# Tile 0's six projections beside the MLP's end: six whole accumulators in place of 24 single units

## The chip, the cores and the metric

The kernel runs on one core of a Trainium2 chip. The metric is the device time of one execution in microseconds. The times given are medians over several executions of the same program.

## The reference

The program adds two branches over the same input `x` of 2048 rows and 512 columns, mixed by a gate.

```python
g = sigmoid((x * gate_w).sum(-1, keepdims=True))
a = A(x, mem0, Wq, Wk, Wv, Wo, seg_len=32)      # recurrent attention with memory, 32 heads of 128
b = gelu(layernorm(x) @ w1 + b1) @ w2 + b2      # MLP, 512 -> 1376 -> 512
return g * a + (1 - g) * b

# A: for each of the 64 segments of 32 rows
h = concat([mem, xs])                           # 8 memory rows + 32 rows of x
q, k, v = h @ Wq, h @ Wk, h @ Wv                # 32 heads of 128 each
o = softmax(mask(q k^T * scale)) v @ Wo
mem, out = o[:8], o[8:]                         # the memory goes on to the next segment
```

The 64 segments are strictly one after the other, because each needs the memory rows of the one before. The MLP has no such order.

## The kernel before

**Two parts, one after the other.** The first part is the whole MLP with the gates. The second part is the recurrent attention, segment by segment. Both are written out under a manual schedule: each engine runs its instructions in the order in which the program text issues them, and the framework adds the waits.

**The MLP's loop.** Rows are taken in 16 tiles of 128, two tiles to a block, so there are 8 blocks (`NBLK`). The hidden width of 1376 is cut into 11 chunks (`FC`, the last of them with 96 rows). The loop over `u` has 88 steps, one for each pair of block and chunk. A step issues `up(u)` (four matmuls of 128 x 256 on L456 into `hp`, which has two buffers, and a Gelu on ScalarE, L461, into `hg`), and then `down(u - 2)` (two matmuls of 128 x 512 on L473 into the accumulators `bp`). At chunks 5 and 7 a step also transposes a normalised tile on TensorE (L445, `tp`). When a block's last `down` is done, VectorE (L476) and ScalarE (L481) write its two rows of `c_all`. The last ScalarE write at the MLP's end releases the first matmul of the second part (L360, the mask).

**A segment in the second part.** The array holds 32 rows of a segment. To use it well, projections are column-tiled: `qk_unit` and `v_unit` issue four matmuls with 32 columns of weights each (L211, L222; 128 rows by 32 columns, moving 512 elements) to the four column groups of the array. One such group of four is called a unit here. An accumulator (one bank of 128 x 512) is complete after four units, one for each 128 rows of the 512-long contraction (`KC` = 4).

**The leftover rows of tile 0.** Only 24 of a segment's 32 rows ride with the 8 memory rows in one column group of 32. The 8 remaining rows of each of the four segments of a tile are gathered into `GL`, 32 rows for a tile, and projected for the whole tile ahead of time: two accumulators for V (`left_v`, `vb` = 0 and 1) and four for Q and K (`left_qk`). In the second part, this work for tile T+1 is filled in during tile T by a generator. For tile 0 it has to be done before the second part starts. This is what `setup()` does. It is a generator, and the MLP's loop calls `next(pre, None)` once per step in the last three blocks (`u` from 55).

- First, `setup()` transposes the memory `m0` with four small matmuls (L488) and gathers the rows with GpSimd (`x_left`, `prep_h`).
- `left_v(0, vb)` yields after each unit. Once complete, an accumulator is written to `vt` by ScalarE (L282), stored to the DRAM tile `vd` by a DMA issued by SyncE (L285), and, after the second one, read back in another order into `vs` by 16 small DMAs (L292). `vt` has one buffer.
- `left_qk(0, t, hf)` yields after each unit too. VectorE then transposes the accumulator (L217) into `Tt` (two buffers in this part), and GpSimd copies it into `QL` (L264) or `KL` (L268).
- `left_v_in(0)` copies `vs` to `VL` on GpSimd (L299).

All six accumulators use one bank of PSUM, since `side()` has one bank here (`nside` = 1). The evacuation is put in a queue by `later` and issued by `flush`, which is called one step of the generator after the last unit. Before it hands out the bank again, `side()` flushes whatever is still queued. With 24 unit yields, six yields after the flushes and one at the start, `setup()` runs from u = 55 to u = 86. Step 87 calls it no more.

**DMA queue.** SyncE issues nearly all DMAs in program order. The second half of `Wo` (L138) is issued in step 74, because it overwrites the staged input `x_all`; it stands in SyncE's order behind the 16 reads of `vs`.

Of the kernel before, what the change touches and what calls it, by code (L numbers as in the profile page):

```python
# [23 lines left out]
def kernel(ctx, tc, A_x, A_mem0, A_Wq, A_Wk, A_Wv, A_Wo, A_seg_len, B_x, B_w1, B_b1, B_w2, B_b2, gate_w, out):  # L24
    nc = tc.nc
    P = 128
    _, S, Dm = A_x.shape
# [109 lines left out]
    def ld_wo(h0, h1):  # L137
        nc.sync.dma_start(Wo_sb[:, h0:h1, :], A_Wo[h0:h1].rearrange("h e d -> e h d"))  # L138
# [45 lines left out]
    def flush(q, n=1):  # L184
        for _ in range(min(n, len(q))):
            k, ev = q.pop(0)
            ev()
            side_todo.discard(k)

    def later(q, ev, k):  # L190
        side_todo.add(k)
        q.append((k, ev))

    def side(shape, dtype=FP32):
        side_n[0] += 1
        n = pools["nside"]
        while side_n[0] - n in side_todo:
            flush(dve_q)
            flush(act_q)
        return bank(5 + side_n[0] % n, shape, dtype)  # L200
# [7 lines left out]
    def qk_unit(bk, G, t, h0, h1, kc):  # L208
        n = (h1 - h0) * 32
        for j in range(4):  # L210
            nc.tensor.matmul(bk[32 * j:32 * j + 32, 0:n], lhsT=G[:, kc, :], rhs=W5[t][:, kc, h0:h1, j, :],  # L211
                             start=(kc == 0), stop=(kc == KC - 1), tile_position=(0, 32 * j))

    def qk_tr(bk, h0, h1):
        n = (h1 - h0) * 32
        Tt = pools["sb"].tile([P, 512], FP32, tag="Tt", bufs=pools["nTt"], name="Tt")
        nc.vector.transpose(out=Tt[:, 0:n], in_=bk[:, 0:n])  # L217
        return Tt[:, 0:n].rearrange("p (h r) -> p h r", r=32)

    def v_unit(bk, G, vb, kc):  # L220
        for j in range(4):
            nc.tensor.matmul(bk[32 * j:32 * j + 32, :], lhsT=G[:, kc, :], rhs=Wv5[:, kc, 4 * vb:4 * vb + 4, j, :],  # L222
                             start=(kc == 0), stop=(kc == KC - 1), tile_position=(0, 32 * j))
# [20 lines left out]
    def x_left(T):  # L244
        xT = xTs[T]
        GL = xp.tile([P, KC, 32], BF16, tag="GL", name="GL")
        nc.gpsimd.tensor_copy(out=GL[:].rearrange("p k (i c) -> p k i c", c=LEFT),
                              in_=xT[:].rearrange("p k (i c) -> p k i c", c=seg)[:, :, :, RIDE:seg])
        GLs[T] = GL
# [3 lines left out]
    def left_qk(T, t, hf):  # L253
        h0, h1 = HF[hf]
        bk = side([P, 512])
        side_k = side_n[0]
        for kc in range(KC):
            qk_unit(bk, GLs[T], t, h0, h1, kc)
            if kc < KC - 1:
                yield  # L260
        def ev():
            Tv = qk_tr(bk, h0, h1)
            if t == 0:
                nc.gpsimd.tensor_copy(out=QL[T % 2][:, h0:h1, :], in_=Tv)  # L264
            else:
                for hh in range(h0 // 8, h1 // 8):
                    r0 = 8 * hh - h0
                    nc.gpsimd.tensor_copy(out=KL[T % 2][:, :, :, hh, :], in_=Tv[:, r0:r0 + 8, :].rearrange("p g (s c) -> p g s c", c=LEFT))  # L268
        later(dve_q, ev, side_k)
        yield  # L270

    def left_v(T, vb):
        bk = side([P, 512])
        side_k = side_n[0]
        for kc in range(KC):
            v_unit(bk, GLs[T], vb, kc)
            if kc < KC - 1:
                yield

        def ev():  # L280
            vt = pools["sb"].tile([P, 4, Dh], BF16, tag="vt", bufs=1, name="vt")
            nc.scalar.copy(out=vt[:].rearrange("p i e -> p (i e)"), in_=bk[:])  # L282
            if vb == 0:
                vds[T] = dr.tile([P, 4, 2, Dh], BF16, tag="vd", name="vd")
            nc.sync.dma_start(vds[T][:, 2 * vb:2 * vb + 2], vt[:].rearrange("p (a g) e -> p a g e", g=2))  # L285
            if vb == 1:
                src = vds.pop(T)[:].rearrange("(j s c) h g e -> j h c s (g e)", j=4, s=SPT)
                vs = pools["sb"].tile([P, SPT, 2, Dh], BF16, tag="vs", bufs=1, name="vs")
                for j in range(4):
                    for hh in range(4):  # L290
                        r0 = 32 * j + LEFT * hh
                        nc.sync.dma_start(vs[r0:r0 + LEFT].rearrange("p s g e -> p s (g e)"), src[j, hh])  # L292
                vls[T] = vs

        later(act_q, ev, side_k)
        yield

    def left_v_in(T):
        nc.gpsimd.tensor_copy(out=VL[T % 2][:], in_=vls.pop(T)[:])  # L299
# [48 lines left out]
    def prep_h(s):  # L348
        T, si = divmod(s, SPT)
        nc.gpsimd.tensor_copy(out=hT[s % NHT][:, :, M:32], in_=xTs[T][:, :, si * seg:si * seg + RIDE])  # L350
# [43 lines left out]
    NBLK = NT // TB  # L394
# [56 lines left out]
    def up(u):  # L451
        blk, fc = divmod(u, FC)
        rows = min(P, F - fc * P)
        hp = mps.tile([P, TB * P], FP32, tag="hp", bufs=2, name="hp")
        for kc in range(KC):
            nc.tensor.matmul(hp[:rows, :], lhsT=w1_sb[:, kc, fc * P:fc * P + rows], rhs=yTs[blk][:, kc, :], start=(kc == 0), stop=(kc == KC - 1))  # L456
        if fc == FC - 1:
            hg_ = hgl[blk % 2]
        else:
            hg_ = mwork.tile([P, TB * P], BF16, tag="hg", bufs=LAG + 2, name="hg")  # L460
        nc.scalar.activation(out=hg_[:rows, :], in_=hp[:rows, :], func=ACTF.Gelu_apprx_tanh, bias=b1_sb[:rows, fc:fc + 1], scale=1.0)  # L461
        return hg_
# [3 lines left out]
    def down(u, hg_):  # L466
        blk, fc = divmod(u, FC)
        rows = min(P, F + 1 - fc * P)
        for tt in range(TB):
            T = blk * TB + tt  # L470
            if fc == 0:
                bpt[T] = mps.tile([P, Dm], FP32, tag=f"bp{T % 4}", name="bp")
            nc.tensor.matmul(bpt[T][:], lhsT=hg_[:rows, tt * P:(tt + 1) * P], rhs=w2_sb[:rows, fc, :], start=(fc == 0), stop=(fc == FC - 1))  # L473
        if fc == FC - 1:
            T = blk * TB
            nc.vector.tensor_scalar(out=c_all[:, T, :], in0=bpt.pop(T)[:], scalar1=omg_all[:, T:T + 1], scalar2=None, op0=ALU.mult)  # L476
            c_q.append(T + 1)

    def c_act():
        for T in c_q:  # L480
            nc.scalar.activation(out=c_all[:, T, :], in_=bpt.pop(T)[:], func=ACTF.Copy, scale=omg_all[:, T:T + 1])  # L481
        c_q.clear()

    def setup():

        m0p = side([P, KC, M], BF16)
        for kc in range(KC):
            nc.tensor.transpose(m0p[:, kc, :], m0[:, kc * P:(kc + 1) * P], ident[:M, :M])  # L488
        nc.vector.tensor_copy(out=hT[0][:, :, 0:M], in_=m0p[:])
        x_left(0)  # L490
        x_left(1)
        prep_h(0)
        yield
        for vb in range(2):
            yield from left_v(0, vb)
            flush(act_q)
            yield
        for hf in range(2):
            for t in range(2):
                yield from left_qk(0, t, hf)  # L500
                flush(dve_q)
                yield
        left_v_in(0)
# [21 lines left out]
    for u in range(NBLK * FC):  # L525
        blk, fc = divmod(u, FC)
        T1 = (blk + 1) * TB
        pend.append((u, up(u)))
        if fc == 2:
            c_act()  # L530
        if len(pend) > LAG:
            down(*pend.pop(0))
        if T1 < NT:
            if fc == 1 or fc == 3:
                ys[fc // 2] = norm(T1 + fc // 2)
            elif fc == 5 or fc == 7:
                norm_tr(T1 + fc // 2 - 2, ys[fc // 2 - 2])
        if blk % 2 == 0:
            if fc in (2, 5, 6, 7) and T1 + 2 < NT:
                bn(T1 + 2 + (2, 5, 6, 7).index(fc) )  # L540
            if fc == 8 and T1 + 2 < NT:
                newton(T1 + 2, T1 + 6)

        elif fc in (2, 4, 6, 8):
            T = T1 + (fc - 2) // 2
            if T < NT:
                gates(T, T + 1)
        elif fc == 10 and T1 < NT:
            gates2(T1, T1 + 4)
        if blk == 0 and fc in (9, 10):  # L550
            gates(fc - 9, fc - 8)
        if blk == 1 and fc == 0:
            gates2(0, 2)
        if blk == 1 and fc in (1, 3):
            gates(2 + fc // 2, 3 + fc // 2)
        if blk == 1 and fc == 9:
            gates2(2, 4)
        if blk == NBLK - 2 and fc == 8:
            ld_wo(H // 2, H)
        if blk >= NBLK - 3:  # L560
            next(pre, None)
    for a in pend:
        down(*a)
# [298 lines left out]
```

## Time and profile before

| | |
|---|---|
| median of 10 executions | 838.2 us (836.77 to 838.51) |
| profiled execution, its own time | 838.28 us |
| its span in the trace | 836.5 us |
| the MLP's last three blocks with `setup()`, first `hp` matmul of u = 55 to the end of the last `bp` matmul | 62.63 to 103.99 us |
| first matmul of the second part (L360) | 104.76 us |
| TensorE busy over the span | 808.7 us (97%) |
| ScalarE, VectorE, GpSimd busy | 434.1, 502.3, 273.6 us |
| granted TensorE clock, mean | 0.998 |

Times in the trace are microseconds from the start of the span. The profiled execution took 1.78 us longer than its span, and lies 0.08 us above the median. A matmul's record is longer than its share of TensorE's time, since matmuls overlap; what a group of matmuls costs is read from start to start.

### The profile page before, as it was taken

Reading aid. Unit: us, or ns where it says so; the run is one execution under the profiler, and the core shown is the slowest. Engines: PE = TensorE matmul, PEld = TensorE weight load, DVE = VectorE, ACT = ScalarE, POOL = GpSimd, SP = SyncE. Lnnn points to the kernel's source line nnn. Section 1 sums busy time; section 2 is a strip of 40 time slices with the busy share of each in tenths; the row PEclk is TensorE's granted clock in tenths of the full one; section 3 lists DMA queues with packets and bytes.
Section 4 is the critical chain, followed back from the end, with each engine's and each line's share of the span. In section 5 each row is a group of like instructions: output and inputs, shape, how many; then the busy total and the mean of one; then the engine's idle time right before and its main releaser. Section 6 shows DMA issues by size and latency. Waiting matters only on the chain.

```text
span 836.5 us, 49253 instructions
## 1 busy us (share of the span) xinstructions
PE 808.7 (97%) x22417; PEld 494.0 (59%) x22417; DVE 502.3 (60%) x1019; ACT 434.1 (52%) x1245; POOL 273.6 (33%) x625
## 2 busy tenths in 40 slices
PE   5999999999999999999999999999999999999986
PEld 3665555666566566656655665666566656655554
DVE  5763256575666666665656565666666565656553
ACT  3554455545455555555455545555554555455542
POOL 8000134242433333243424242423333243424220
PEclk9999999999999999999999999999999999999999
DMA  9890300000001010101010100001010101010000
GB/s 307 276 377 24 103 25 15 24 16 15 25 18 28 10 36 9 37 11 35 4 31 15 29 17 21 25 18 28 10 36 11 36 10 35 4 35 6 10 5 24
DMA packets 38216, 37.64 MB, mean 45 GB/s; under 512 B 13545, under 2 KB 36434, under 8 KB 36466
## 3 DMA queue, kind: packets, MB, share of 16 engines
q1 hardware_dynamic: 37874, 34.31, 12.4%
q8 instruction: 177, 2.90, 1.4%
q14 instruction: 37, 0.30, 0.1%
q0 software_dynamic: 128, 0.13, 0.1%
HBM read 26.03 MB, written 6.29 MB: 39 GB/s over the span
## 4 chain that ended last, share of the span: by engine, by line
PE 94%; DVE 2%; DMA 1%; SPq 1%; ACT 1%; issue 1%; DVEq 0%; ACTq 0%
PE b L211 35%; PE b L233 18%; PE b L222 17%; PE b L384 5%; PE hp L456 4%; PE bp L473 4%; PE b L360 2%; PE b L369 2%; PE b L681 2%; PE b L716 1%; PE b L389 1%; PE b L670 1%; DMA Wo_sb<-in_A_x_dram 1%; PE b L320 1%; PE b L373 0%
## 5 line engine op out<-in xcount | busy, mean ns | idle before, releaser
L217 DVE STREAM_TRANSPOSE Tt<-b 128x512 f32<-128x512 f32 (+1 forms) x384 | 225.9, 614 | 86.7 <-PE b L211 72.5
L211 PEld LDWEIGHTS <-hT 128*32 128x32 bf16 x5120 | 134.8, 97 | 100.2 <-DVE hT L717 15.5
L233 PE MATMUL b<-Wo_sb,UTT 128*32 128x256 bf16 (+1 forms) x4736 | 162.7, 285 | 1.2 <-ACT UTT L616 0.8
L222 PE MATMUL b<-Wv_sb,hT 128*32 128x512 bf16 x2048 | 141.8, 378 | 0.0
L211 PE MATMUL b<-Wq_sb,hT 128*32 128x512 bf16 x2048 | 132.9, 379 | 1.4 <-DVE hT L717 1.4
L211 PE MATMUL b<-Wk_sb,hT 128*32 128x256 bf16 (+1 forms) x3072 | 133.4, 308 | 0.0
L233 PEld LDWEIGHTS <-UTT 128*32 128x32 bf16 x4736 | 121.3, 97 | 19.3 <-ACT UTT L616 1.5
L651 ACT CAST KT<-Tt 128x256 bf16<-128x256 f32 (+1 forms) x192 | 87.1, 476 | 53.9 <-DVE Tt L217 53.8
L602 POOL TENSOR_TENSOR Px<-E,R 128x256 bf16<-128x256 bf16 x64 | 43.0, 672 | 219.4 <-DVE R L686 219.4
L686 DVE RECIPROCAL R<-b 128x256 f32<-128x256 f32 x64 | 112.5, 1758 | 0.0
L651 POOL CAST QT<-Tt 128x512 bf16<-128x512 f32 x64 | 39.1, 611 | 192.2 <-DVE Tt L217 192.2
L616 ACT CAST UTT<-b 128x256 bf16<-128x256 f32 x256 | 76.9, 388 | 23.5 <-PE b L389 23.5
L705 ACT CAST wsb<-b 128x256 bf16<-128x256 f32 x66 | 24.6, 372 | 120.0 <-PE b L233 120.0
L674 DVE RECIPROCAL R<-b 128x64 f32<-128x64 f32 x64 | 35.7, 557 | 79.5 <-PE b L671 79.5
L651 ACT CAST QT<-Tt 128x512 bf16<-128x512 f32 x64 | 39.6, 619 | 65.5 <-DVE Tt L217 65.5
L384 PEld LDWEIGHTS <-V 32*128 32x128 bf16 x4096 | 35.2, 91 | 45.7 <-DVE Pm L676 31.8
L222 PEld LDWEIGHTS <-hT 128*32 128x32 bf16 x2048 | 49.5, 96 | 21.1
L461 ACT ACTIVATE hg<-hp,b_sb 128x256 bf16<-128x256 f32 x80 | 37.7, 473 | 44.8 <-PE hp L456 44.6
L685 ACT CAST UTT<-b 128x64 bf16<-128x64 f32 x128 | 20.9, 215 | 75.0 <-PE b L389 75.0
L456 PE MATMUL hp<-yT,w_sb 128*128 128x256 bf16 (+1 forms) x352 | 54.0, 278 | 3.4 <-ACT hg L461 1.6
L604 POOL TENSOR_TENSOR racc<-racc,R 128x320 f32<-128x320 f32 x64 | 55.5, 867 | 0.0
L717 DVE CAST hT<-b 128x32 bf16<-128x32 f32 x63 | 12.1, 192 | 62.0 <-PE b L716 62.0
(116 smaller groups left out, 1079.0 us busy)
## 6 DMA issues: line engine op xcount, KB each, us to landing
Wv_sb<-in_A_Wv_dram SPq DMA_DIRECT2D x4, 1024.0 KB
Wq_sb<-in_A_Wq_dram SPq DMA_DIRECT2D x4, 1024.0 KB
Wk_sb<-in_A_Wk_dram SPq DMA_DIRECT2D x4, 1024.0 KB
Wo_sb<-in_A_Wo_dram SPq DMA_DIRECT2D x2, 2048.0 KB
vd<-vt SPq DMA_DIRECT2D x32, 128.0 KB
vs<-vd SPq DMA_DIRECT2D x256, 16.0 KB
out_dram<-o SPq DMA_DIRECT2D x16, 128.0 KB
Wo_sb<-in_A_x_dram SPq DMA_DIRECT2D x1, 1024.0 KB
```

Of the source, the lines that this page charges most:

```text
L211: nc.tensor.matmul(bk[32 * j:32 * j + 32, 0:n], lhsT=G[:, kc, :], rhs=W5[t][:, kc, h0:h1, j, :], start=(kc == 0), stop=(kc == KC - 1), til ...
L217: nc.vector.transpose(out=Tt[:, 0:n], in_=bk[:, 0:n])
L222: nc.tensor.matmul(bk[32 * j:32 * j + 32, :], lhsT=G[:, kc, :], rhs=Wv5[:, kc, 4 * vb:4 * vb + 4, j, :], start=(kc == 0), stop=(kc == KC - ...
L233: nc.tensor.matmul(bk[32 * g:32 * g + 32, :], lhsT=ut[:, i, j, c0:c0 + 32], rhs=Wo_sb[:, 4 * i + j, d0:d1], start=(j == 0 and i < 4), stop ...
L384: nc.tensor.matmul(U[j][:, i, :], lhsT=V[q, i, :], rhs=Pt[q, i, c_main:c_main + n], start=(i == 0), stop=False, skip_group_check=True, til ...
L456: nc.tensor.matmul(hp[:rows, :], lhsT=w1_sb[:, kc, fc * P:fc * P + rows], rhs=yTs[blk][:, kc, :], start=(kc == 0), stop=(kc == KC - 1))
L461: nc.scalar.activation(out=hg_[:rows, :], in_=hp[:rows, :], func=ACTF.Gelu_apprx_tanh, bias=b1_sb[:rows, fc:fc + 1], scale=1.0)
L602: nc.gpsimd.tensor_tensor(out=Px[:, :, 0:32], in0=E[:, :, 16:48], in1=Rr, op=ALU.mult)
L604: nc.gpsimd.tensor_tensor(out=racc[:], in0=racc[:], in1=R[:], op=ALU.add)
L616: nc.scalar.copy(out=UTT[T % 2][:, :, j, c0 + M:c0 + 40], in_=U[:])
L651: (nc.gpsimd.tensor_copy if bi == 2 else nc.scalar.copy)(out=dst, in_=Tv)
L686: nc.vector.reciprocal(out=R[:, 8 * NG:].rearrange("p (i q) -> p i q", q=32), in_=sr)
```

## The change

The generators `left_v` and `left_qk` are run through without yielding, so all four units of an accumulator (16 matmuls) are issued one after the other, and its evacuation is flushed right behind them in the same step. The loop now calls `next(pre, None)` at every fourth step only. The yields that remain are one at the start and one for each of the six accumulators; the calls come at u = 56 (memory transposes), 60 and 64 (V), 68, 72, 76 and 80 (Q and K, in the same order as before), and 84 (`left_v_in`).

```diff
@@ setup()
         for vb in range(2):
-            yield from left_v(0, vb)
+            for _ in left_v(0, vb):
+                pass
             flush(act_q)
             yield
         for hf in range(2):
             for t in range(2):
-                yield from left_qk(0, t, hf)
+                for _ in left_qk(0, t, hf):
+                    pass
                 flush(dve_q)
                 yield
         left_v_in(0)
@@ the MLP's loop over u
-        if blk >= NBLK - 3:
+
+        if blk >= NBLK - 3 and u % 4 == 0:
             next(pre, None)
```

No instruction is added or taken away on TensorE, ScalarE, GpSimd or SyncE, and the order on GpSimd and SyncE stays as it was. On VectorE, some transposes of L217 change places with the normalisation (L438, L446) and the writes of `c_all` (L476).

## Prediction

> **What bounds the kernel now.** I read the page first, for the engine that sets the pace.
>
> ```profile
> PE 808.7 (97%) x22417; PEld 494.0 (59%) x22417; DVE 502.3 (60%) x1019; ACT 434.1 (52%) x1245; POOL 273.6 (33%) x625
> PE   5999999999999999999999999999999999999986
> PEclk9999999999999999999999999999999999999999
> PE 94%; DVE 2%; DMA 1%; SPq 1%; ACT 1%; issue 1%; DVEq 0%; ACTq 0%
> ```
>
> TensorE is busy in every slice but the first and the last two, at its full clock, and holds 94% of the chain that ended last. So time saved on TensorE shows at the end if nothing else becomes late. A busy record does not say that the array works at its best, so I went to the timeline of TensorE in the stretch that the change touches. Columns are start, duration, engine, line, operation. First steps without a unit, then with one, then whole accumulators where the second part begins:
>
> ```profile
> 54.80 0.59 PE L473 MATMUL bp<-w_sb,hg 128*128 128x512 bf16 x2
> 55.23 0.60 PE L456 MATMUL hp<-yT,w_sb 128*128 128x256 bf16 x4
> 55.67 0.59 PE L473 MATMUL bp<-w_sb,hg 128*128 128x512 bf16 x2
> ...
> 57.41 0.59 PE L473 MATMUL bp<-w_sb,hg 128*128 128x512 bf16 x2
> ...
> 77.39 0.40 PE L211 MATMUL b<-Wq_sb,GL 128*32 128x512 bf16 x4
> 77.72 0.61 PE L456 MATMUL hp<-yT,w_sb 128*128 128x256 bf16 x4
> 78.17 0.60 PE L473 MATMUL bp<-w_sb,hgl 97*128 97x512 bf16 x2
> 78.70 0.40 PE L211 MATMUL b<-Wq_sb,GL 128*32 128x512 bf16 x4
> ...
> 81.31 0.40 PE L211 MATMUL b<-Wq_sb,GL 128*32 128x512 bf16 x4
> ...
> 105.04 1.05 PE L211 MATMUL b<-Wq_sb,hT 128*32 128x512 bf16 x16
> 105.92 1.04 PE L211 MATMUL b<-Wk_sb,hT 128*32 128x512 bf16 x16
> 106.78 1.04 PE L211 MATMUL b<-Wq_sb,hT 128*32 128x512 bf16 x16
> 107.64 1.05 PE L211 MATMUL b<-Wk_sb,hT 128*32 128x256 bf16 x32
> ```
>
> A plain step takes (57.41 - 54.80) / 3 = 0.87 us, a step with one unit (81.31 - 77.39) / 3 = 1.307 us: a lone unit costs 0.437 us. In an unbroken run, three accumulators take 107.64 - 105.04 = 2.60 us, or 0.217 us per unit. Half of a lone unit's price is thus no work: it is lost at the two changes between full-width weights (128*128) and column tiles (128*32). The rows place it: from `bp` (78.17) to the unit (78.70) there are 0.53 us, against 0.43 us from `bp` (54.80) to `hp` (55.23) in a plain step, and from the unit to the next `hp` 0.33 us, against 0.217 in a run. That is some 0.10 us going in and 0.12 coming out. No row calls it a wait; the records run into each other.
>
> **The change part by part.**
>
> *Lone units become runs.* Before, 24 units each stand between full-width matmuls: 24 x 0.437 = 10.49 us. As a check, from `hp` of u = 55 (62.63) to `hp` of u = 87 (102.09) there are 39.46 us; less 32 plain steps (27.84), four groups of `tp` transposes at 0.22 (0.88) and the memory transposes (0.27), 10.47 us remain. After, six runs stand there, and each pays the two changes once: 0.437 + 3 x 0.217 = 1.088 us, so 6.53 us in all. The saving is 10.49 - 6.53 = 3.96 us, or 18 pairs of changes at 0.22 us. The order of the compiled kernel has the sixteen matmuls of each accumulator without anything between them, and `tp` or `bp` ahead and `hp` behind, all full-width.
>
> For the price of a pair of changes there is also a rule. The Trainium skill, "TensorEngine Tiling (Array Packing)", Key Properties, says that changing the tiling mode drains the engine; "TensorE: Matmul & The Clock Gate", Single matmul latency, gives a drain as about 166 ns on a warm array. An estimate from these pages, two drains a pair, is 18 x 0.332 = 6.0 us, and so 832.3 us. The rows show 0.10 and 0.12 us instead, and they decide.
>
> *The run itself.* Its rate inside the MLP is not in the trace. The nearest row is the run of the second part, the same instruction on `hT` in place of `GL`, both 32 columns wide, from the same weights: 0.217 us per unit. The other end is that every unit costs 0.437 as now, a saving of nothing. I take the row.
>
> *Weights.* V's first unit moves from u = 56 to 60 and Q's from 66 to 68, K's from 71 to 72: all later in steps, with no wait for them before. Later accumulators come sooner by up to five steps, on weights already in use. Cost nothing.
>
> *Evacuation on ScalarE.* The copies to `vt` now stand directly behind the last unit of their step, so they wait for it, and the Gelu of the next step is queued behind them.
>
> ```profile
> 69.70 0.47 ACT L461 ACTIVATE hg<-hp,b_sb 128x256 bf16<-128x256 f32 x1 [0.83 <-PE hp L456]
> 70.08 0.58 ACT L282 CAST vt<-b 128x512 bf16<-128x512 f32 x1
> 70.80 0.47 ACT L461 ACTIVATE hg<-hp,b_sb 128x256 bf16<-128x256 f32 x1
> ```
>
> The next step's `hp` takes 0.6 us after the run, about as long as the copy (0.58). The Gelu starts at most some 0.1 us late, and its result is used two steps, 1.74 us, later. `hp` has two buffers. No cost.
>
> *The second `vt` copy waits for a DMA.* `vt` has one buffer, so copy two needs the first store to `vd` done. The stores now lie closer: four steps plus a `tp` group and one run, 3.48 + 0.22 + 1.09 = 4.79 us between run ends, where the copies lay 76.67 - 70.08 = 6.59 us apart. The first store is issued 0.6 us after its copy starts (70.68), and the DMA rows in half-microsecond windows (last columns: share and GB/s) show when it moves:
>
> ```profile
> 71.00:71.50 0.50, 0.50 (x6) 0.22 (x6) 0.33 (x2) 0.27 (x1) 0.00 (x0) 1.00 0.00 0
> 71.50:72.00 0.50, 0.50 (x5) 0.39 (x5) 0.00 (x0) 0.00 (x0) 0.00 (x0) 1.00 0.74 262
> 72.00:72.50 0.50, 0.50 (x7) 0.31 (x4) 0.00 (x0) 0.40 (x1) 0.00 (x0) 1.00 0.00 0
> ```
>
> It has moved by 72.0, 1.3 us after issue; with 0.7 us for the notice (an estimate; SyncE's longest wait on `vd` was 0.7) it is done 2.6 us after its copy starts, 2.2 us before it is needed. Another bound is the slowest 128 KB in the trace, `gw_bc`, 6.9 us from issue to landing under a full load of DMA at the start. The copy would then wait 6.9 + 0.6 - 4.8 = 2.7 us, with Gelus queued behind it. TensorE has some 2 us until `hp` has no free buffer or `down` lacks `hg`, so 0.7 to 0.9 us would be lost. I take zero and keep 0.9 for the range.
>
> *Evacuation on VectorE.* Each transpose (0.72 us) now waits for its run. Behind the one of step 68 stands the second `y` (L438), which its `tp` needs in step 73, some 4 us later; behind the one of step 72 the second `yT` copy, which the MLP needs in step 77. The third transpose also waits for GpSimd to free `Tt`, copied 0.61 us after the first, two accumulators earlier. The single PSUM bank is wanted again 2.6 us or more after a run ends, and is free after 0.1 + 0.72. A rule that speaks against the change is in the page on tiling, PSUM Bottleneck: faster column tiles can make the evacuation the bottleneck. Rows of 0.58 and 0.72 us against at least 2.6 do not let it bind here; were the copies unhidden, six times about 0.7, or 4.2 us, would cancel the saving.
>
> *SyncE and GpSimd.* The sixteen `vs` reads and the second half of `Wo` follow the second store, which by my step times moves from 77.3 to about 74.9. `Wo` then lands near 88.7 instead of 91.1 and is needed at about 108.9 (112.85 now). GpSimd's last copy before the join, `VL`, runs at 102.0 now and at some 96 after; it had no waiter. So the second part is released, as now, by the last `c_all` on ScalarE:
>
> ```profile
> 104.03 0.69 ACT L481 ACTIVATE c_all<-bp,omg_all 128x512 bf16<-128x512 f32 x1 [0.82 <-PE bp L473]
> ```
>
> That follows the last `bp`, moves with it, and what stands behind it (table load, first transposes, segments) moves as one block.
>
> *Sum.* 838.28 - 3.96 = 834.32 us for a profiled execution. Its median lies 0.08 lower: 834.24, which I give as 834.3.
>
> **The rivals.**
>
> *A: the run does not run faster, or the saving is given back at the join.* If units still cost 0.437, or if something not moved by the change (a DMA, `VL`) released the second part, the time stays near 838.2. For it: the run at 0.217 is seen only in the second part. Against it: same instruction form and same weights, and slack of some 20 us for `Wo` and several for `VL`. Half of it would give 836.2. Chance 5%.
>
> *B: the second `vt` copy waits long, and the time ends above.* Place: ScalarE, step 64. Once the store takes more than about 6 us, each further microsecond stops TensorE. From 6 + 3.96 = 10 us on it outweighs the saving, from 11.6 on it shows as slower; at 13.8, twice the slowest row, the time would be 834.3 + 7.8 = 842.1. For it: one buffer, and Gelus queued behind. Against it: 1.3 us of transfer on queues with a DMA share of zero just before. Chance 2%.
>
> *C: the changes cost more than single starts show.* If overlap hid part of the plain steps' work, the saving could be 0.25 us a pair, 4.5 us, and 833.7. Chance 5%, inside the range.
>
> **How the numbers follow.** Forecast with C: 93%. The ten runs before lie from 1.4 below to 0.3 above their median, so I allow 0.6 us for a median. Above: 834.3 + 0.9 (ScalarE) + 0.6 = 835.8; below: 833.7 with 0.3 of scatter, 833.4. About 0.2%, 1.7 us, is what a measurement of this kernel can tell from no change; faster means under 836.5. Forecast, C and part of A are faster: 0.94. The rest of A is the same: 0.04. B is slower: 0.02.
>
> **What would show it.** Right: sixteen matmuls of L222 starting near 68.4, steps with a run of about 1.96 us from `bp` to `bp`, no idle row on TensorE before `hp` with ScalarE as releaser, the last `bp` ending near 100.0 and the mask matmul near 100.8, and the second part as long as before (836.5 - 104.76 = 731.7 us). Wrong: runs of 1.7 us or more from start to the next `hp`; idle time on TensorE at steps 65 to 67 ended by ScalarE; or a second part longer by what the first saved.

## The result, and the profile after

| | before | after |
|---|---|---|
| median | 838.03 us (28 executions) | 835.06 us (834.36 to 835.99, 8 executions) |
| ratio of the times | | 0.9966, 95% interval 0.9957 to 0.9975 |
| profiled execution, its own time | 838.28 us | 834.30 us |
| its span | 836.5 us | 832.5 us |
| first `hp` of u = 55 to the mask matmul L360 | 104.76 - 62.63 = 42.13 us | 100.88 - 62.70 = 38.18 us |
| mask matmul to the end of the span ("second part" below) | 731.74 us | 731.62 us |

The kernel became faster. The forecast of 834.3 us is 0.8 us below the median, inside the range of 833.4 to 835.8. In the pair of profiled executions the saving is 3.98 us, of which 3.95 lie in the MLP's end. Between the medians it is 2.97 us (by the interval 2.1 to 3.6). That the pair shows the whole saving is in part chance: the profiled execution of the changed kernel is the fastest of the ten on record, 0.76 us below the median. Two later executions, one of the kernel before and one of pairs, took 2681 us and are left out of the ratios. Where the last microsecond went is the question of the later experiments.

From the page of the changed kernel:

```profile
PE 804.9 (97%) x22417; PEld 494.2 (59%) x22417; DVE 502.1 (60%) x1019; ACT 433.9 (52%) x1245; POOL 273.7 (33%) x625
PE   5999999999999999999999999999999999999986
PEclk9999999999999999999999999999999999999998
PE 93%; DVE 3%; DMA 1%; SPq 1%; ACT 1%; issue 1%; DVEq 0%; ACTq 0%
```

The matmuls are the same 22417, but TensorE's busy time has gone down from 808.7 to 804.9 us. TensorE was counted as busy while it changed between full-width weights and column tiles: the 3.8 us were never shown as a wait. The timeline of TensorE in the changed kernel shows a step with a run, and the join:

```profile
77.36 0.59 PE L473 MATMUL bp<-w_sb,hg 128*128 128x512 bf16 x2
77.89 1.05 PE L211 MATMUL b<-Wq_sb,GL 128*32 128x512 bf16 x16
78.87 0.61 PE L456 MATMUL hp<-yT,w_sb 128*128 128x256 bf16 x4
79.31 0.59 PE L473 MATMUL bp<-w_sb,hg 128*128 128x512 bf16 x2
...
99.50 0.60 PE L473 MATMUL bp<-w_sb,hgl 97*128 97x512 bf16 x2
100.88 0.35 PE L360 MATMUL b<-MkA,ident 128*128 128x448 bf16 x1 [0.78 <-ACT c_all L481]
101.16 1.05 PE L211 MATMUL b<-Wq_sb,hT 128*32 128x512 bf16 x16
```

From `bp` to the run there are 0.53 us and from the run to `hp` 0.98 us. A lone unit took 0.53 and 0.33. So three further units cost 0.65 us, 0.217 each. The step takes 79.31 - 77.36 = 1.95 us, and the join waits 0.78 us for ScalarE, as before. ScalarE's rows for the two V copies:

```profile
69.62 0.59 ACT L282 CAST vt<-b 128x512 bf16<-128x512 f32 x1 [1.11 <-PE b L222]
70.21 0.47 ACT L461 ACTIVATE hg<-hp,b_sb 128x256 bf16<-128x256 f32 x1
...
74.44 0.58 ACT L282 CAST vt<-b 128x512 bf16<-128x512 f32 x1 [0.94 <-PE b L222]
```

Both copies wait for their run, as the prediction had it, and the second one for nothing else: the store had been reported. No wait of TensorE stands between 60 and 100 us.

### The profile page after: what moved, and what is told of

Read it like the earlier page. It is cut to its first block, busy times and chain, and to the rows that moved or that the text cites. A ratio compares the mean times of both kernels' runs of the same rounds, so it can differ in the third digit from the quotient of the medians.

```text
span 832.5 us, 49251 instructions
## 1 busy us (share of the span) xinstructions
PE 804.9 (97%) x22417; PEld 494.2 (59%) x22417; DVE 502.1 (60%) x1019; ACT 433.9 (52%) x1245; POOL 273.7 (33%) x625
## 4 chain that ended last, share of the span: by engine, by line
PE 93%; DVE 3%; DMA 1%; SPq 1%; ACT 1%; issue 1%; DVEq 0%; ACTq 0%
PE b L211 35%; PE b L233 18%; PE b L222 17%; PE b L384 5%; PE hp L456 4%; PE bp L473 4%; PE b L360 2%; PE b L369 2%; PE b L684 2%; PE b L719 1%; PE b L389 1%; PE b L673 1%; DMA Wo_sb<-in_A_x_dram 1%; PE b L320 1%; PE b L373 0%
## 5 line engine op out<-in xcount | busy, mean ns | idle before, releaser
L217 DVE STREAM_TRANSPOSE Tt<-b 128x512 f32<-128x512 f32 (+1 forms) x384 | 225.7, 614 | 85.4 <-PE b L211 71.8
```

## The experiments

Twelve runs in three groups of four, each group beside the kernel before on the same chip (medians 838.43, 838.51 and 838.47 us; the runs have 5 to 12 executions each). "To the mask" is the time from the first `hp` of u = 55 to the mask matmul, "second part" the rest of the span, both of the profiled execution.

| kernel | to the mask, us | second part, us | median, us | ratio to before, 95% interval |
|---|---|---|---|---|
| before, again | 42.13 | 732.88 | 839.0 | 1.0003 (0.9993 to 1.0012) |
| after, again | 38.17 | 732.78 | 835.40 | 0.9969 (0.9958 to 0.9980) |
| pairs | 39.50 | 734.44 | 837.33 | 0.9987 (0.9977 to 0.9997) |
| split pairs | 42.15 | 732.54 | 839.18 | 1.0014 (1.0005 to 1.0022) |
| V accumulators close | 38.15 | 733.19 | 835.07 | 0.9954 (0.9940 to 0.9968) |
| last run at the join | 38.18 | 730.82 | 835.12 | 0.9954 (0.9941 to 0.9968) |
| after, one VectorE instruction more | 38.17 | 733.32 | 835.20 | 0.9957 (0.9943 to 0.9970) |
| after, nine more | 38.18 | 732.16 | 834.61 | 0.9949 (0.9936 to 0.9963) |
| after, nine more, again | 38.17 | 732.38 | 834.29 | 0.9951 (0.9937 to 0.9965) |
| before, eight more | 42.13 | 731.48 | 837.96 | 0.9991 (0.9982 to 1.0000) |
| two runs of three | 37.27 | 732.12 | 833.55 | 0.9942 (0.9929 to 0.9956) |
| two runs of three, eight more | 37.27 | 732.71 | 833.60 | 0.9937 (0.9923 to 0.9950) |

For the same work in the MLP's end the first column repeats within 0.03 us; the second spreads over more than 3 us. That alone says where the cause of the saving can be read, and where the scatter is.

### Are the changes between weights the cause?

**Pairs.** Units in twelve runs of two, every second step.

```diff
-            for _ in left_v(0, vb):
-                pass
+            for n, _ in enumerate(left_v(0, vb)):
+                if n == 1:
+                    yield
...
-        if blk >= NBLK - 3 and u % 4 == 0:
+        if blk >= NBLK - 3 and u % 2 == 0:
```

(This is against the changed kernel. `left_qk` is changed in the same way.)

> Units in pairs: twelve runs of two units (8 matmuls), one in every second step from u = 58 to 80, evacuations flushed at once as in the changed kernel. Theory (each pair of changes between full-width weights and column tiles costs 0.22 us): 12 of the 24 pairs of changes go, 2.64 us, so the mask matmul 2.6 us earlier than in the kernel before and 1.3 us later than in the changed one; a run of two units costs 0.437 + 0.217 = 0.654 us. Rival (what helps is fewer interrupted steps, or the evacuation being issued earlier, not the neighbours of a unit): the same 2.6 us, so this run alone does not tell them apart; the next one does.

**Split pairs.** The same steps and flushes, but one unit ahead of `down` and one behind it; for this the generators yield after each of an accumulator's first three units (`n < 3` in place of `n == 1`). Against pairs:

```diff
+        if blk >= NBLK - 3 and u % 2 == 0 and u > 56:
+            next(pre, None)
         if len(pend) > LAG:
             down(*pend.pop(0))
...
         if blk >= NBLK - 3 and u % 2 == 0:
             next(pre, None)
```

> The same steps, the same units per step and the same flushes as in pairs, but the two units of a step stand apart: one between up and down, one behind down. Theory of changes between weights: 24 lone units again, so no saving: the mask matmul where it is in the kernel before, within 0.2 us, and 2.6 us later than in pairs. Rival (number of interrupted steps, or time of evacuation): as fast as pairs, 2.6 us below the kernel before.

TensorE's timeline in pairs:

```profile
65.89 0.59 PE L473 MATMUL bp<-w_sb,hg 128*128 128x512 bf16 x2
66.42 0.62 PE L222 MATMUL b<-Wv_sb,GL 128*32 128x512 bf16 x8
66.97 0.61 PE L456 MATMUL hp<-yT,w_sb 128*128 128x256 bf16 x4
67.42 0.59 PE L473 MATMUL bp<-w_sb,hg 128*128 128x512 bf16 x2
```

and in split pairs:

```profile
65.51 0.60 PE L456 MATMUL hp<-yT,w_sb 128*128 128x256 bf16 x4
66.04 0.40 PE L222 MATMUL b<-Wv_sb,GL 128*32 128x512 bf16 x4
66.37 0.61 PE L473 MATMUL bp<-w_sb,hg 128*128 128x512 bf16 x2
66.91 0.40 PE L222 MATMUL b<-Wv_sb,GL 128*32 128x512 bf16 x4
67.24 0.61 PE L456 MATMUL hp<-yT,w_sb 128*128 128x256 bf16 x4
```

A pair takes 0.55 us to the next `hp`, two lone units 0.33 each, and each of these has its own way in. Pairs reach the mask 2.63 us earlier than the kernel before (2.64 expected), split pairs at the same place (42.15). The steps, the units per step and the evacuations are alike in the two, so it is the neighbours of a unit that count: a change into column tiles and out of them costs 0.22 us. The rival is out. The prediction's estimate from the two pages of the skill (0.332 us a pair) would have given pairs 4.0 us, and the changed kernel 6.0; the runs give 2.63 and 3.95. The 166 ns that it took for a drain are the whole constant of a lone matmul's latency, which by the same section has the issue and other parts in it.

The medians of these two do not follow their first column: pairs are 1.1 us below the kernel before instead of 2.6, split pairs 0.8 us above it (1.2 by the ratio) instead of equal.

### Does the second V copy wait for its store?

**V accumulators close.** Steps 60 and 61 in place of 60 and 64.

```diff
-        if blk >= NBLK - 3 and u % 4 == 0:
+        if blk >= NBLK - 3 and u in (56, 60, 61, 68, 72, 76, 80, 84):
```

> The changed kernel with the two V accumulators one step apart (steps 60 and 61) instead of four: a test of the wait of the second copy to vt for the first store, which was put at 2.6 us after the first copy starts, with some 2 us of cover on TensorE behind it. Theory: the second copy could start 1.96 us after the first and starts 2.4 to 2.8 us after it, Gelus behind it are late by under 1 us, TensorE does not wait; mask matmul as in the changed kernel, 38.2 us after the first hp of u = 55. Rival (the store is slow to be reported, near the 6.9 us of the first 128 KB transfer of the kernel): the second copy starts about 7 us after the first and TensorE stands for 2 to 3 us in steps 63 to 65.

ScalarE's timeline there:

```profile
69.38 0.58 ACT L282 CAST vt<-b 128x512 bf16<-128x512 f32 x1 [1.11 <-PE b L222]
69.97 0.47 ACT L461 ACTIVATE hg<-hp,b_sb 128x256 bf16<-128x256 f32 x1
71.78 0.58 ACT L282 CAST vt<-b 128x512 bf16<-128x512 f32 x1 [1.34 <-DMA vd<-vt]
```

The second copy starts 2.40 us after the first, and now a DMA ends its wait; the store was issued at 69.99, so issue to report took 1.8 us. The prediction had put 2.6. TensorE did not wait, and the mask came at 38.15 us. In the changed kernel the copies start 4.82 us apart, so 2.4 us of slack remain. The slow-store rival is out for this place.

### Can the wait at the join take a run?

**Last run at the join.** The sixth accumulator behind the last `bp` matmuls.

```diff
             for t in range(2):
+                if hf == t == 1:
+                    left_v_in(0)
                 for _ in left_qk(0, t, hf):
...
-        if blk >= NBLK - 3 and u % 4 == 0:
+        if blk >= NBLK - 3 and u % 4 == 0 and u < 80:
```

> The changed kernel with the sixth accumulator (K, second half) moved behind the MLP's last matmuls, and the copy to VL ahead of it. There TensorE waits 0.78 us for the last write of c_all. Theory: the run costs 1.09 us in the MLP and, behind the last bp, 0.87 + 0.10 for going in, 0.78 of it covered; mask matmul 37.4 us after the first hp of u = 55 instead of 38.2, so 0.8 us saved, if the new evacuation (0.72 on VectorE behind the last c_all, 0.74 on GpSimd) does not hold up the first segment. Rival: the evacuation stands ahead of the first segment's work on VectorE and GpSimd, and the first segment or the mask matmul is later by 0.7 to 1.5 us, so nothing is saved or up to 0.7 us lost.

TensorE's timeline there:

```profile
98.22 0.60 PE L473 MATMUL bp<-w_sb,hgl 97*128 97x512 bf16 x2
98.75 1.05 PE L211 MATMUL b<-Wk_sb,GL 128*32 128x512 bf16 x16
100.68 0.36 PE L360 MATMUL b<-MkA,ident 128*128 128x448 bf16 x1 [0.89 <-DVE Tt L217]
```

The run no longer costs anything in the MLP, but the mask matmul now waits 0.89 us for the transpose of that run, and stands at 38.18 us, where it stood. The rival was right: nothing is saved. The PSUM of the accumulator belongs to a pool of the first part, which the program closes before the second part opens its own, and its last reader is now this transpose. That the mask matmul waits for this memory is read from the program, not tested. The median (835.12) is no argument for this version, since nothing moved in the stretch that was changed.

### Where is the last microsecond?

**Both kernels again.**

> The kernel before, unchanged, beside the others of this group. Question: the two profiled executions differ by 3.98 us, the medians by 2.97 us. Theory (the saving of 3.96 us in the MLP is whole, and the rest is scatter from execution to execution in stretches that the change does not touch): the mask matmul L360 at 104.7 to 104.8 us from the start of the MLP's u = 55 as in the first profile (42.1 us after the first hp of u = 55), ratio 1.000 within 0.1%. Rival (some later part gives back 1 us, and the profiled execution hid it): the stretch after the mask matmul is 1 us shorter here than in the changed kernel.

> The changed kernel, unchanged, with more executions. Theory of scatter: ratio 0.9953 (3.96 us) lies inside the interval, the mask matmul 38.2 us after the first hp of u = 55, and the stretch after the mask matmul within 0.3 us of the kernel before. Rival (1 us given back): ratio near 0.9965 again with an interval that leaves out 0.9953, and a stretch after the mask matmul that is 1 us longer.

Neither expectation came out whole. The MLP again gives 3.96 us in the profiled pair, and the two second parts differ by 0.1 us. But the medians again differ by 3.0 us only, and the interval again leaves out 0.9953. The unchanged kernel itself has medians of 838.43 and 839.0 us in this group, so half a microsecond between medians is scatter. So I took the second part apart. Start to start of the mask matmul is the length of a segment. Of the 64, 43 repeat within 0.06 us in all fourteen traces; 21 do not, and here are seven of them:

```
segment           0      7     21     28     35  |  42     48
before          9.95  11.51  10.96  11.84  11.21 | 11.03  11.47
before, again   9.95  11.51  10.96  11.83  11.21 | 11.03  11.46
after          10.22  11.21  11.29  11.46  11.56 | 11.58  11.69
after, again   10.22  11.21  11.29  11.46  11.56 | 11.94  11.67
pairs          10.22  11.21  11.28  11.46  11.56 | 12.13  11.98
split pairs    10.23  11.21  11.29  11.63  11.56 | 11.94  11.70
V close        10.22  11.21  11.29  11.68  11.56 | 11.94  11.68
```

The columns on the left lie a multiple of seven segments apart. (Others, such as 11, 18, 25 and 45, differ by 0.2 to 0.6 us between two traces of one and the same kernel.) Segment 0 shows on VectorE what happens. Before:

```profile
110.90 0.56 DVE L674 RECIPROCAL R<-b 128x64 f32<-128x64 f32 x1 [1.64 <-PE b L671]
111.56 0.29 DVE L676 TENSOR_TENSOR Pm<-E,R 128x128 bf16<-128x128 bf16 x1
```

and after:

```profile
107.01 0.56 DVE L677 RECIPROCAL R<-b 128x64 f32<-128x64 f32 x1 [1.63 <-PE b L674]
108.03 0.29 DVE L679 TENSOR_TENSOR Pm<-E,R 128x128 bf16<-128x128 bf16 x1 [0.46 <-DVE R L677]
```

The second instruction needs the first, which ended at 107.57, and starts 0.46 us later, with nothing else in the profile to wait for; before, it started 0.10 us later. TensorE waits for it, and the segment is 0.27 us longer. The order of the instructions shows one difference: ahead of the mask matmul VectorE has 161 in the kernel before, waits included, and 160 in the changed one, because the new order spares a wait. The traces, which hold 21 more VectorE records up to there, agree: 182 and 181. TensorE's weight loads and waits go from 697 to 696 records. So each of the two engines has one wait fewer, which "The change" does not say. That gave a theory, and a test of it.

**One and nine small VectorE instructions more** (a memset of one column in step 58, with `n` = 1 or 9 in the changed kernel and 8 in the kernel before):

```diff
+        if u == 58:
+            for _ in range(n):
+                nc.vector.memset(pad[:], 0.0)
```

> The changed kernel with one small VectorE instruction more (a memset of one column in step 58, with slack on both sides). Why: in the traces so far the MLP gives the whole saving (2.63 us in pairs, 3.95 in the changed kernel), but the second part is longer in all three changed kernels at the same segments (segment 0 by 0.27 us, 21, 35, 42, 48) and shorter at others (7, 28), every seventh segment; the three have one VectorE instruction fewer ahead of the second part than the kernel before, a wait on a second semaphore that the new order spares. Theory (stalls that return at a fixed number of VectorE instructions, moved by one place): with the count restored, segment 0 takes 9.95 us again instead of 10.22, segment 7 about 11.5, segments 21 and 35 about 10.95 and 11.2; MLP as in the changed kernel (38.2 us from the first hp of u = 55 to the mask matmul); median 0.5 to 1 us below the changed kernel. Rival (scatter, or the state in which the MLP leaves the second part): segment 0 stays at 10.22, and the median within 0.3 us of the changed kernel.

> The same with nine small VectorE instructions in step 58, which moves everything behind by about half a segment's worth (some 18 to 23 VectorE instructions, waits included). Theory of stalls at a fixed number of VectorE instructions: the set of slow segments changes again, segment 0 takes 9.95 us, and stalls stand at other places in a segment; the sum over the second part may go either way by 1 to 2 us. MLP unchanged: 38.2 us. Rival: the same slow segments as in the changed kernel.

> The kernel before with eight small VectorE instructions in step 58: again 169 ahead of the mask matmul. Theory (the slow segments are set by the number of VectorE instructions, whatever the MLP's end looks like): segments 0, 7, 21, 28 and 35 take 9.94, 11.21, 10.94, 11.46 and 11.21 us, as in the changed kernel with nine; mask matmul at 42.13 us after the first hp of u = 55. Compared with the changed kernel at the same count (next run), the medians then differ by the MLP's 3.95 us, within 0.6. Rival (the runs in the MLP leave the second part slower by about 1 us in some other way): they differ by about 3 us, and segments 42 and 48, which were longer in every changed kernel, are 11.03 and 11.47 us here.

> The changed kernel with nine small VectorE instructions once more, on the same chip as the kernel before with eight: same count of 169 on both. Theory: 3.95 us below that kernel's median, within 0.6, and segments 0, 7, 21, 28, 35 alike. Rival: 3 us below.

```
VectorE ahead     segment   0      7     21     28     35  |  42     48
161  after, one more      9.94  11.51  10.96  11.83  11.21 | 11.19  11.96
161  two runs             9.94  11.51  10.96  11.83  11.20 | 11.36  11.65
169  after, nine more     9.94  11.21  10.94  11.46  11.21 | 11.50  11.69
169  the same, again      9.95  11.21  10.95  11.67  11.21 | 11.20  11.74
169  before, eight more   9.95  11.22  10.94  11.46  11.21 | 11.03  11.69
169  two runs, eight      9.95  11.21  10.94  11.47  11.21 | 11.16  12.16
```

One instruction more gives back the kernel before, column by column on the left. In VectorE's timeline of that run:

```profile
106.81 0.56 DVE L681 RECIPROCAL R<-b 128x64 f32<-128x64 f32 x1 [1.63 <-PE b L678]
107.47 0.29 DVE L683 TENSOR_TENSOR Pm<-E,R 128x128 bf16<-128x128 bf16 x1
```

In segments 0, 7, 21 and 35, kernels with the same count have the same slow segments, whatever the end of their MLP looks like. So these stalls belong to the place in VectorE's instruction stream, and the rival (the state that the MLP leaves) is out for them. Segment 28 follows the count less well: split pairs, V close and the second trace of nine more stand 0.2 us above the others of their count, and that last one is the same program as the first. (The version with the last run at the join is not listed; its VectorE stream differs behind the mask as well.)

It does not explain the whole microsecond. Over the five columns on the left the changed kernel gains and loses nearly the same: +0.27, +0.33 and +0.35 against -0.30 and -0.38, so 0.27 us in all. Segments 42 and 48 go their own way. Segment 42 takes 11.03 us in all three traces of the kernel before, eight VectorE instructions more or not, and 11.16 to 12.13 in the eleven others: this half of the rival in the expectation came true. Segment 48 did not follow it (11.69 us with eight more, as in the changed kernel). In the repeated run of the changed kernel, TensorE itself stands within segment 42:

```profile
571.31 0.22 PE L384 MATMUL b<-Px,V 32*128 32x32 bf16 x7 [0.41 <-issue]
```

where the kernel before runs all 32 of these matmuls in one go:

```profile
574.70 0.37 PE L384 MATMUL b<-Px,V 32*128 32x32 bf16 x32
```

At equal counts the medians differ by 3.3 us at 161 (838.51 against 835.20) and by 3.7 us at 169 (837.96 against 834.29), on one chip each. The expectation of 3.95 within 0.6, stated for 169, holds there. But the restored count did not bring the 0.5 to 1 us that was expected of it. The changed kernel did not run on that chip; the version with V close did, with the same time to the mask and the changed kernel's slow segments 0, 21 and 35, and its median is 835.07, no slower than 835.20. So the placement of these stalls is shown segment by segment, and that it makes up the missing microsecond is not; with some five executions of each and half a microsecond of scatter, the medians can't tell. What sets segments 42 and 48 is open. For 42, TensorE's own stream is a candidate: only the kernel before has the one wait more on TensorE. No run changed that count alone.

### A further step

**Two runs of three accumulators** (steps 69 and 81), in banks of `bp` that are idle then.

```diff
+        if alt[0] is not None:
+            return mps.tile(shape, dtype, tag=f"bp{alt[0]}", name="bp")
         return bank(5 + side_n[0] % n, shape, dtype)
...
+        for n, (f, args) in enumerate(((left_v, (0,)), (left_v, (1,)), (left_qk, (0, 0)), ...)):
+            alt[0] = (None, 2, 3, None, 0, 1)[n]
+            for _ in f(0, *args):
+                pass
+            if n % 3 == 2:
+                flush(act_q, 9)
+                flush(dve_q, 9)
+                alt[0] = None
+                yield
...
-        if blk >= NBLK - 3 and u % 4 == 0:
+        if u in (56, 69, 81, 84):
```

> A further step along the change: two runs of three accumulators (48 matmuls each, at steps 69 and 81) instead of six runs of one. The second and third accumulator of a run use banks of bp that are idle then (2 and 3 in block 6, 0 and 1 in block 7). Theory (0.22 us for each pair of changes between full-width weights and column tiles): four more pairs go, 0.88 us, so the mask matmul 37.3 us after the first hp of u = 55 instead of 38.18 (42.13 in the kernel before). The second vt copy waits for the first store, 2.4 us after the first copy, which the two units and steps behind it cover. Rival (evacuations become the bound when three accumulators come at once: three transposes of 0.72 us, two copies on ScalarE with a DMA between them): TensorE waits at steps 70 to 72 for Gelus behind the second copy, 0.5 to 1.5 us, and the mask matmul is at 38 us or later.

> The same with eight small VectorE instructions in step 58, so that 169 VectorE instructions, waits included, lie ahead of the mask matmul, as in the run with nine of them on the changed kernel. Theory: MLP as in two_runs, 37.3 us; segments 0, 7, 21, 28 and 35 as in that run (9.94, 11.21, 10.94, 11.46, 11.21 us); of all kernels here the lowest median, about 0.9 us below the changed kernel with nine, near 833.7. Rival: the slow segments go with what the MLP does, and this kernel has other ones.

TensorE's timeline in two runs:

```profile
76.27 1.05 PE L225 MATMUL b<-Wv_sb,GL 128*32 128x512 bf16 x16
77.14 1.04 PE L225 MATMUL bp<-Wv_sb,GL 128*32 128x512 bf16 x16
78.00 1.04 PE L214 MATMUL bp<-Wq_sb,GL 128*32 128x512 bf16 x16
78.97 0.61 PE L459 MATMUL hp<-yT,w_sb 128*128 128x256 bf16 x4
```

and ScalarE's row of the second copy:

```profile
79.78 0.59 ACT L285 CAST vt<-bp 128x512 bf16<-128x512 f32 x1 [1.83 <-DMA vd<-vt]
```

ScalarE stands 1.83 us for the store, and TensorE does not notice. Inside a run the accumulator changes twice (77.14, 78.00) and the projection once (from V to Q), at 0.86 to 0.87 us from start to start, four units at 0.217: so it is not a new accumulator or a new operand that costs, but the change of tile shape. The mask comes at 37.27 us: 0.91 saved where 0.88 was expected. Both versions have the lowest medians of all, 833.55 and 833.60, about 4.9 us below the kernel before. The expected slow segments came too, and so did a median near 833.7 for the padded one, 0.7 us below the changed kernel with nine more; but it is no lower than the unpadded one's. An extra 1.6 us stood in its segment 1 in the profiled execution, where no other kernel has it.

## Why the prediction was right

- **The price of a pair of changes, 0.22 us, and so 3.96 us for eighteen.** Right: 3.95 in the first pair of traces, 3.96 in the second, 2.63 for the twelve pairs that the pairs version spares, 0.91 for the four more that two runs spare, and nothing when as many lone units stood closer together.
- **The rate in a run, 0.217 us a unit, taken from the second part.** Right: 0.98 us from run to `hp` against 0.33 for one unit, so 0.65 for three.
- **Evacuations cost nothing.** Right: no wait on TensorE. The store was reported after 1.8 us (with the V accumulators close), against an estimate of 2.0 and a bound of 6.9; the 0.9 us kept for the range were not needed.
- **The join moves with the last `bp`.** Right: mask matmul at 100.88, 100.8 forecast, behind the same 0.78 us.
- **"What stands behind it moves as one block."** This is the step that was off. It held in the two pairs of profiled executions, within 0.1 us, but not in the medians; the pairs were in part luck, as the first profiled execution of the changed kernel is the fastest of its ten. The second part is no block: its length went from 730.82 to 734.44 us over fourteen traces, and one instruction less on VectorE moved stalls of 0.3 us by place. The term was put at zero with 0.6 us of scatter around the median; it measured about 1 us in the unfavourable direction. The median lies inside the range because the range was wide enough, not because this term was right; where the microsecond comes from stays open.
- **The rivals.** A's premise, that units in a run are no faster, did not hold. B's wait exists, but is 2.4 us short of mattering. C's cheaper case did not come.

## What to carry to other kernels

A busy matmul engine can hide lost time: compare start-to-start times of the same instruction alone and in a run before taking 97% busy for an engine at its limit. Work that is mixed in between other matmuls is better mixed in blocks when its weights have another tile shape. Here the size of a block was bounded by the idle PSUM banks; the evacuation did not stop TensorE even with three accumulators at once. When a gain in one stage and the medians disagree, cut the rest of the trace at a marker that recurs and compare piece by piece.

## What was not expected of the hardware

Adding or sparing one small VectorE instruction early in the program moves stalls of 0.27 to 0.38 us to other instructions hundreds of microseconds later, in segments 0, 7, 21 and 35 alike in every trace with the same count. They stand a multiple of seven segments apart, and VectorE has 126 to 131 records, waits included, in seven segments. The page's queue of small instruction transfers (`q14 instruction`) holds 37 packets with 0.30 MB; the DMA records give 8192 bytes for each. The Trainium skill, "Perfetto Trace Analysis", The 4-stage abstract model, says that instructions have 64 bytes, so that such a packet would hold 128 of them. This fits stalls at the borders of fetched blocks.

The DMA records of the traces speak for it too. In segment 0 one of these packets starts 7.8 to 8.1 us after the mask matmul in the five traces at 160, 5.1 us in the four at 161 and 2.6 us in the four at 169: it moves with VectorE's count. At 160 it follows the stalled instruction, which starts at 7.15 us. At 161 it falls in the 1.6 us in which VectorE waits for TensorE anyway (4.5 to 6.1 us), and no stall shows there. Which engine a packet serves is not in the record, and no run moved the border without moving the instructions, so the mechanism is argued, not shown.
